# Decoding two weight tiles of an MLP during the attention that stands before it

## The chip, the cores and the metric

The kernel runs on one core of one Trainium2 chip, in one launch. The metric is the device time of one execution in microseconds; lower is better. Three executions of the kernel before took 1065.11, 1061.65 and 1064.87 us, the median is 1064.87 us.

The engines are called by their names in the profile: PE is TensorE (matrix products), DVE is VectorE, ACT is ScalarE, POOL is GpSimd, and SP is the queue that issues all DMA transfers here.

## The reference

Attention with a feature map of exponentials, then two mixer blocks, each of which mixes tokens and then channels. Cut to what is computed:

```python
def phi(x):                      # 64 -> 256 features
    proj = einsum('bhsd,df->bhsf', x, w_phi)
    proj = proj - max(abs(proj), axis=-1)
    return concatenate([exp(proj), exp(-proj)], axis=-1)
num = phi(q) @ (phi(k).T @ v)    # 4 batches, 8 heads, 576 tokens, 64 wide
den = phi(q) @ sum(phi(k)) + 1e-6
x = heads_side_by_side(num / den)            # 4 x 576 x 512
u  = x + (x.T @ U @ V).T                     # token mix, rank 32
x  = u + relu(u @ w_ch1) @ w_ch2             # first channel MLP, 512 -> 2048 -> 512
u2 = x + (relu(x.T @ w_tok1) @ w_tok2).T     # token mix, 576 -> 256 -> 576
out = u2 + relu(u2 @ w2_ch1) @ w2_ch2        # second channel MLP, 512 -> 1536 -> 512
```

## The kernel before, in words

**Numbers.** Every product is made with operands that are split into a high and a low part, and is the sum of three: high by high, high by low, low by high. All weights of the MLPs and mixes reach the chip as 64-bit words. `load64` brings one half tile (128 x 512 words, 512 KB) by DMA into a buffer `raw` (L148) and makes single precision of it: two ACT instructions write `w` and `r` (L153, L154), two DVE instructions join them (L156, L159). `load_half` then calls `split`: ACT casts the high part (`wh`, L99), POOL or DVE subtracts for the low part (`wl`, L104). One weight tile of a hidden slice is two such halves, one for the up and one for the down product, each with a high and a low part.

**Stages.** Stage A works on 16 pairs of heads (4 batches of 4 pairs), one pair in five rounds. A table of rounds (`at(r, fn)`) holds the calls in program order: projections, `k1` to `k3` for the keys, `q1` and `q2` for the queries, `x0`, `xr` and `x1` for the division (the denominators go through DRAM, `rD` and `rec`, L405 to L418), then per batch the rank-32 token mix (`tm0`, `tm1`, `tm2`) and the first 5 of the 16 hidden slices of the first channel MLP (`ma_u`, `ma_h`, `ma_y`), whose weights `a0` to `a4` stand in the pool `wring`. Results go to DRAM as `uD` and `sD`. The last batch's mix and MLP part run after the last heads. `uha`, `ula` and `hp_a` belong to that part, `uhb`, `ulb`, `hp_b` and `yb` to stage B.

Stage B takes the other 11 slices (`b0` to `b10`) for eight half batches of 288 tokens (`channel`), and after each second half `tokmix2`, the second block's token mix; names there are `gp`, `gh`, `gl`, `m2p`, and `x2` is the sum, which goes to DRAM as `u2D`. The first tiles have a pool of their own each (`wrB0` ...), the last ones reuse `wring`. Stage B's decoding of the first READY=8 tiles is issued behind the last `rec` transfer (`tc.issue_after(recl[0])`).

Stage C is the second channel MLP in five chunks of 256 and four times 512 tokens (`channelC`). Its weights are made by `pair_weights` for six pairs of slices, `sh`, `sl` (up) and `vh`, `vl` (down) for each, in pools `wc0` to `wc5` that lie where stage B's pools on the right-hand side lay, so each waits for the last reader of what it lies over. The first chunk, with `u0c`, `u1c`, `hpc`, `hhc`, `hlc`, `yc`, takes the pairs in order as they are decoded; the later ones use combinations of quarters (`t0c` to `t6c`, `u2c`, `xc`).

**Order.** Nothing runs in the order in which the calls stand: a scheduler in the build lays out each engine's instructions by its own simulated times, with the calls' order as priority. `issue_after` holds a call back behind a named instruction. Each engine then works its list strictly in order.

Of the kernel before, what the change touches and what calls it, by code (L numbers as in the profile page):

```python
# [30 lines left out]
NF1 = 16  # L31
NF2 = 12
NA = 5
NR = NF2 - NA
EPS = 1e-06
CHUNKS = (256, 512, 512, 512, 512)
HM = 256
EARLY = 2
READY = 8


NF32 = 4
# [50 lines left out]
def body(ctx, tc, kq, vd, w_phi, U, V, wm1, wt1, wt2, wm2, out):  # L93
# [12 lines left out]
    def split(src, hi, lo, eh, el):  # L106
        cp(eh, hi, src)
        sub(el, lo, src, f32(hi))
# [24 lines left out]
    AB = ExitStack()  # L133
    stage = AB.enter_context(tc.tile_pool(name="stage", bufs=RAWB))
    mlp = AB.enter_context(tc.tile_pool(name="mlp", bufs=2))
    wring = AB.enter_context(tc.tile_pool(name="wring", bufs=NA))

    halves, extra = [], []

# [24 lines left out]
    def load_half(src, i, name, k, hi, lo):  # L164
        sl = slice(k * C, (k + 1) * C)
        w = load64(src[i][:, sl], P, C, f"{name}_{k}")
        split(w, hi[:, sl], lo[:, sl], WHI[name[0]][k], WLO[name[0]][k])

    def w_tiles(pool, name, slot=""):
        return [pool.tile([P, 2 * C], F32R, tag=f"{t}{slot}", name=f"{t}_{name}") for t in ("wh", "wl")]  # L170

    def load_w(pool, src, i, name, slot=""):
        hi, lo = w_tiles(pool, name, slot)
        for k in range(2):
            load_half(src, i, name, k, hi, lo)
        return hi, lo
# [69 lines left out]
    def at(r, fn, *args):  # L246
        rounds.setdefault(r, []).append((fn, args))
# [153 lines left out]
    recs, pks, subs, exps = {}, {}, [], []  # L401
# [75 lines left out]
    def load_wa(f, k):  # L477
        if k == 0:
            wA.append(w_tiles(wring, f"a{f}"))
        with tc.issue_after(subs[-1]), tc.issue_after(exps[-1]):  # L480
            load_half(wm1, f, f"a{f}", k, *wA[f])

    uhl, hss, ys = {}, {}, {}

    def ma_u(b, ch):
# [45 lines left out]
    at(O_MIX, mix_consts)  # L531
    for h in range(2 * NA):
        at(O_WA + (h * D_WA) // 2, load_wa, h // 2, h % 2)
    span = 5 * NPAIR
    for b in range(B):
        r = span * b + 5 * (NPAIR - 1) + O_TM
# [17 lines left out]
    with tc.using_default_side("right"):  # L554
        wrB = [BX.enter_context(tc.tile_pool(name=f"wrB{f}", bufs=1, reuse_waits="tile")) for f in range(NR)]
        extra.append(BX.enter_context(tc.tile_pool(name="rawx", bufs=RAWX, reuse_waits="tile")))
# [6 lines left out]

    nB = NF1 - NA
    def load_b(f):
        if f < NR:
            return load_w(wrB[f], wm1, NA + f, f"b{f}", f)
        return load_w(wring, wm1, NA + f, f"b{f}")

    with tc.issue_after(recl[0]):  # L570
        wB = [load_b(f) for f in range(READY)]

# [59 lines left out]
    def load_u(src, nm, *where):  # L632
        u = mlp.tile(list(src.shape), F32, tag="xT", name=f"u{nm}")
        nc.sync.dma_start(u, src)
        uh, ul = split_u(u, nm, *where)
        return u, uh, ul
# [3 lines left out]
    def mix2_consts():  # L640
        T1H = bc.tile([P, NT, 256], F32R, name="T1H")
        T1L = bc.tile([P, NT, 256], F32R, name="T1L")
        for t in range(NT):
            w = load64(wt1[:, t], P, 256, f"t1_{t}")
            split(w, T1H[:, t], T1L[:, t], "v", "v")
        T2H = bc.tile([P, 2, S], F32R, tag="T2H", name="T2H")
        T2L = bc.tile([P, 2, S], F32R, tag="T2L", name="T2L")
        for j in range(2):
            for k in range(2):
                sl = slice(k * N, (k + 1) * N)  # L650
                w = load64(wt2[:, j, sl], P, N, f"t2_{j}_{k}")
                split(w, T2H[:, j, sl], T2L[:, j, sl], "v", "v")
        return T1H, T1L, T2H, T2L

    for b in range(B):
        x2 = b2.tile([P, NC, S], F32, tag="x2", name=f"x2_{b}", bufs=1)
        for ch in range(2):
            nm = f"b{b}_{ch}"
            i = 2 * b + ch
            u, uh, ul = load_u(uD[i], nm) if i else u0  # L660
            xc = x2[:, :, ch * N : (ch + 1) * N]
            nc.sync.dma_start(xc, sD[i])
            nc.vector.tensor_add(xc, xc, u)
            channel(wB, uh, ul, xc, xc, nm)
            if i == 0:
                T1H, T1L, T2H, T2L = mix2_consts()
        tokmix2(b, x2, T1H, T1L, T2H, T2L)

# [277 lines left out]
```

## Time and profile before

| | us |
|---|---|
| median of three executions | 1064.87 |
| lowest, highest | 1061.65, 1065.11 |
| the profiled execution | 1064.01 |
| its span, from first to last instruction | 1062.2 |
| busy PE, DVE, ACT, POOL | 1015.5, 631.5, 448.5, 240.2 |
| mean granted clock of PE | 0.988 |

The profiled execution spends 1.81 us outside its span. Stage A's heads end near 356 us, the last batch's mix follows until about 385, stage B ends near 770, and stage C fills the rest. A row of a timeline names the start, the length, the engine, the line, the operands (output before the arrow) and in brackets how long the engine was idle before and what ended that. Instructions of one engine overlap a little, so the distance of two starts can be shorter than a length.

### The profile page before, as it was taken

What the parts mean: (1) busy time and instruction counts of PE and PEld (TensorE: products, weight loads), DVE (VectorE), ACT (ScalarE), POOL (GpSimd) and SP (SyncE); (2) the same over time, 40 slices, a digit from 0 to 9 for tenths busy, and PEclk for the clock granted to TensorE, in tenths of its full rate; (3) what the DMA queues carried; (4) which work ended last, traced back from release to release, by engine and by line L of the source; (5) the groups of instructions that cost most, each with busy time, mean ns of one, the idle gap of its engine ahead of it and who ended that gap; (6) DMA issues with size and microseconds to landing.
All of it is one profiled execution on the core that took longest, in us unless ns stands there. A gap on an engine that the chain in (4) does not pass through costs nothing.

```text
span 1062.2 us, 17389 instructions
## 1 busy us (share of the span) xinstructions
PE 1015.5 (96%) x6828; PEld 948.6 (89%) x6828; DVE 631.5 (59%) x1117; ACT 448.5 (42%) x1039; POOL 240.2 (23%) x186
## 2 busy tenths in 40 slices
PE   8988999899989799999999999999899999999998
PEld 6767899799989689999999999998898898988897
DVE  6778867786686596834223323327888763644633
ACT  6766665655655567522112012115673321312211
POOL 3217655555555134100000000003260000000000
PEclk9999999999999899999999999999899999999999
DMA  7532331232231587410300300202753030020201
GB/s 217 159 101 64 106 89 55 81 90 81 73 100 57 169 270 240 125 60 11 102 23 1 112 23 2 89 1 86 249 157 109 2 102 18 19 102 1 80 1 40
DMA packets 59266, 92.15 MB, mean 87 GB/s; under 512 B 14512, under 2 KB 38832, under 8 KB 59184
## 3 DMA queue, kind: packets, MB, share of 16 engines
q1 hardware_dynamic: 59184, 91.03, 27.3%
q8 instruction: 54, 0.88, 0.4%
q14 instruction: 28, 0.23, 0.1%
HBM read 71.99 MB, written 18.95 MB: 86 GB/s over the span
## 4 chain that ended last, share of the span: by engine, by line
PE 75%; DVE 9%; ACT 6%; DMA 4%; issue 3%; POOL 2%; SPq 1%; ACTq 0%; DVEq 0%; POOLq 0%
PE yc L111 14%; PE yb L111 11%; PE hp_b L111 11%; PE pp L111 5%; PE hp_a L111 4%; PE yp L111 4%; PE nm L111 4%; PE kvp L111 3%; PE vc L111 3%; PE zc L111 3%; PE xc L111 3%; PE m2p L111 2%; DMA raw_a<-in_wm_dram 2%; PE gp L111 2%; DVE w_b L159 1%
## 5 line engine op out<-in xcount | busy, mean ns | idle before, releaser
L194 ACT ACTIVATE hhb<-hp_b 128x288 fp32r<-128x288 f32 x88 | 35.9, 408 | 198.2 <-PE hp_b L111 195.5
L195 DVE SCALAR_TENSOR_TENSOR hlb<-hp_b,hhb 128x288 fp32r<-128x288 f32 x88 | 40.0, 455 | 129.1 <-ACT hhb L194 129.1
L111 PE MATMUL hp_b<-ulb,wh_b 128*128 128x288 f32 x352 | 104.0, 296 | 0.0
L111 PE MATMUL hp_b<-uhb,wl_b 128*128 128x288 f32 x352 | 104.0, 296 | 0.0
L111 PE MATMUL hp_b<-uhb,wh_b 128*128 128x288 f32 x352 | 103.4, 295 | 0.0
L111 PE MATMUL yb<-hlb,wh_b 128*128 128x288 f32 x352 | 97.9, 298 | 2.9 <-DVE hlb L195 2.7
L104 POOL TENSOR_TENSOR sl<-w_c,sh 128x256 fp32r<-128x256 f32 (+1 forms) x18 | 23.5, 1326 | 326.3 <-ACT sh L99 326.3
L111 PE MATMUL yb<-hhb,wl_b 128*128 128x288 f32 x352 | 97.1, 295 | 0.0
L111 PE MATMUL yc<-hlc,vh 128*128 128x512 f32 (+1 forms) x240 | 88.6, 373 | 0.0
L111 PE MATMUL yc<-hhc,vl 128*128 128x512 f32 (+1 forms) x240 | 88.3, 373 | 0.0
L111 PE MATMUL pp<-KW,kq 128*128 128x256 f32 x320 | 82.5, 384 | 2.2 <-issue 1.3
L111 PE MATMUL yc<-hhc,vh 128*128 128x512 f32 (+1 forms) x240 | 81.0, 373 | 0.0
L104 POOL TENSOR_TENSOR qel<-qe,qeh 128x640 fp32r<-128x640 f32 (+1 forms) x48 | 70.1, 1468 | 35.7 <-DVE qeh L101 25.1
L286 DVE TENSOR_REDUCE km<-pp 128x4 f32<-128x512 f32 x80 | 54.9, 686 | 28.1 <-PE pp L111 27.7
L111 PEld LDWEIGHTS yb<-hlb,wh_b 128*128 128x128 f32 x352 | 66.1, 188 | 4.8 <-DVE hlb L195 4.7
L111 PE MATMUL yb<-hhb,wh_b 128*128 128x288 f32 x352 | 67.5, 296 | 0.1
L111 PEld LDWEIGHTS hp_b<-ulb,wh_b 128*128 128x128 f32 x352 | 66.2, 188 | 0.3
L111 PEld LDWEIGHTS hp_b<-uhb,wh_b 128*128 128x128 f32 x352 | 66.1, 188 | 0.2
L111 PEld LDWEIGHTS yb<-hhb,wl_b 128*128 128x128 f32 x352 | 66.3, 188 | 0.0
L111 PEld LDWEIGHTS pp<-KW,kq 128*128 128x128 f32 x320 | 57.7, 192 | 9.6 <-issue 1.7
L111 PEld LDWEIGHTS hp_b<-uhb,wl_b 128*128 128x128 f32 x352 | 66.1, 188 | 0.0
L104 POOL TENSOR_TENSOR kel<-ke,keh 128x512 fp32r<-128x512 f32 x36 | 51.4, 1438 | 46.4 <-ACT keh L99 41.1
(242 smaller groups left out, 2892.9 us busy)
## 6 DMA issues: line engine op xcount, KB each, us to landing
raw_c<-in_wm_dram SPq DMA_DIRECT2D x24, 512.0 KB, 4.5
raw_b<-in_wm_dram SPq DMA_DIRECT2D x22, 512.0 KB, 5.3
kq<-in_kq_dram SPq DMA_DIRECT2D x80, 128.0 KB, 2.2
raw_a<-in_wm_dram SPq DMA_DIRECT2D x10, 512.0 KB, 4.3
rec<-rD SPq DMA_DIRECT2D x32, 144.0 KB, 3.1
uD<-xT SPq DMA_DIRECT2D x8, 576.0 KB, 4.2
sD<-ys SPq DMA_DIRECT2D x8, 576.0 KB, 3.9
ub<-uD SPq DMA_DIRECT2D x8, 576.0 KB, 3.7
```

Source lines behind the costliest of these rows:

```text
L104: return ENG[e].tensor_tensor(out=o, in0=a, in1=b, op=ALU.subtract)
L111: return nc.tensor.matmul(o, l, r, start=start, stop=stop, skip_group_check=True)
L159: nc.vector.scalar_tensor_tensor(out=wi, in0=top, scalar=-(2**31), in1=wi, op0=ALU.bitwise_and, op1=ALU.bitwise_or)
L194: a = nc.scalar.activation(hh, hp, AF.Relu)
L195: v = nc.vector.scalar_tensor_tensor(out=hl, in0=hp, scalar=0.0, in1=f32(hh), op0=ALU.max, op1=ALU.subtract)
L286: nc.vector.tensor_reduce(out=m, in_=pv, op=ALU.max, axis=AX.X, apply_absolute_value=True)
```

## The change

The pool `wring` grows from 5 to 7 tiles, and the pools `wrB` shrink from 7 to 5. The main tiles b0 and b1 are loaded and decoded by `load_we` in four halves, which stand in the table at rounds 74, 78, 82 and 86, that is during the last two pairs of heads and the mix behind them. Stage B's own loading begins at b2. After the first half batch the list of weights is turned, so that later half batches take b2 to b10 first and b0 and b1 last. The count of decode instructions stays the same.

```diff
--- before.py
+++ after.py
@@ -31,12 +31,15 @@
 NF1 = 16
 NF2 = 12
 NA = 5
-NR = NF2 - NA
+NE = 2
+NR = NF2 - NA - NE
 EPS = 1e-06
 CHUNKS = (256, 512, 512, 512, 512)
 HM = 256
 EARLY = 2
 READY = 8
+O_WB = 74
+D_WB = 4
 
 
 NF32 = 4
@@ -133,7 +136,7 @@
     AB = ExitStack()
     stage = AB.enter_context(tc.tile_pool(name="stage", bufs=RAWB))
     mlp = AB.enter_context(tc.tile_pool(name="mlp", bufs=2))
-    wring = AB.enter_context(tc.tile_pool(name="wring", bufs=NA))
+    wring = AB.enter_context(tc.tile_pool(name="wring", bufs=NA + NE))
 
     halves, extra = [], []
 
@@ -480,6 +483,14 @@
         with tc.issue_after(subs[-1]), tc.issue_after(exps[-1]):
             load_half(wm1, f, f"a{f}", k, *wA[f])
 
+    wE = []
+
+    def load_we(f, k):
+        if k == 0:
+            wE.append(w_tiles(wring, f"b{f}"))
+        with tc.issue_after(subs[-1]), tc.issue_after(exps[-1]):
+            load_half(wm1, NA + f, f"b{f}", k, *wE[f])
+
     uhl, hss, ys = {}, {}, {}
 
     def ma_u(b, ch):
@@ -531,6 +542,8 @@
     at(O_MIX, mix_consts)
     for h in range(2 * NA):
         at(O_WA + (h * D_WA) // 2, load_wa, h // 2, h % 2)
+    for h in range(2 * NE):
+        at(O_WB + h * D_WB, load_we, h // 2, h % 2)
     span = 5 * NPAIR
     for b in range(B):
         r = span * b + 5 * (NPAIR - 1) + O_TM
@@ -563,8 +576,10 @@
 
     nB = NF1 - NA
     def load_b(f):
-        if f < NR:
-            return load_w(wrB[f], wm1, NA + f, f"b{f}", f)
+        if f < NE:
+            return wE[f]
+        if f < NE + NR:
+            return load_w(wrB[f - NE], wm1, NA + f, f"b{f}", f - NE)
         return load_w(wring, wm1, NA + f, f"b{f}")
 
     with tc.issue_after(recl[0]):
@@ -663,6 +678,7 @@
             nc.vector.tensor_add(xc, xc, u)
             channel(wB, uh, ul, xc, xc, nm)
             if i == 0:
+                wB[:] = wB[NE:] + wB[:NE]
                 T1H, T1L, T2H, T2L = mix2_consts()
         tokmix2(b, x2, T1H, T1L, T2H, T2L)
```

What the scheduler makes of it is shown at three places. Buffer numbers stand behind the names, line numbers of the kernel after are larger by 3 and more.

The first is POOL at the last pair of heads (pair 15). `keh`, `qel` are its key and query features, `wl_b` low parts of weights. Before:

```order
L104 TENSOR_TENSOR keh15_4_4241<-ke15_4_4238,keh15_4_4241 64x512
L104 TENSOR_TENSOR qel15_0_0_4264<-qe15_0_0_4260,qeh15_0_0_4263 128x640
L104 TENSOR_TENSOR qel15_1_0_4275<-qe15_1_0_4271,qeh15_1_0_4274 128x640
L104 TENSOR_TENSOR qel15_0_1_4324<-qe15_0_1_4320,qeh15_0_1_4323 128x2x256
L104 TENSOR_TENSOR qel15_1_1_4334<-qe15_1_1_4330,qeh15_1_1_4333 128x2x256
L104 TENSOR_TENSOR wl_b0_5089<-w_b0_0_5092,wh_b0_5088 128x512
L104 TENSOR_TENSOR wl_b0_5089<-w_b0_1_5102,wh_b0_5088 128x512
```

After:

```order
L107 TENSOR_TENSOR keh15_4_4263<-ke15_4_4260,keh15_4_4263 64x512
L107 TENSOR_TENSOR wl_b0_4005<-w_b0_1_4225,wh_b0_4004 128x512
L107 TENSOR_TENSOR qel15_0_0_4286<-qe15_0_0_4282,qeh15_0_0_4285 128x640
L107 TENSOR_TENSOR qel15_1_0_4297<-qe15_1_0_4293,qeh15_1_0_4296 128x640
L107 TENSOR_TENSOR wl_b1_4413<-w_b1_0_4416,wh_b1_4412 128x512
L107 TENSOR_TENSOR qel15_0_1_4346<-qe15_0_1_4342,qeh15_0_1_4345 128x2x256
L107 TENSOR_TENSOR qel15_1_1_4356<-qe15_1_1_4352,qeh15_1_1_4355 128x2x256
L107 TENSOR_TENSOR wl_b1_4413<-w_b1_1_4506,wh_b1_4412 128x512
```

Two weight subtractions now stand among the features of the last pair, one ahead of its first query feature and one ahead of its third.

The second is ACT behind the heads, where `xh3` are the last batch's transposed tokens and `rh3` the cast that the rank-32 mix waits for. Before:

```order
L358 CAST xh3_3_4532<-xp3_3_4527 128x512
L355 CAST xh3_4_4560<-xp3_4_4555 64x512
L154 ACTIVATE r_b2_0_5137<-raw_b2_0_5134 128x512
L153 ACTIVATE w_b1_1_5124<-raw_b1_1_5122 128x512
L99 CAST wh_b1_5110<-w_b1_0_5114 128x512
L154 ACTIVATE r_b2_1_5147<-raw_b2_1_5144 128x512
L99 CAST rh3_4581<-rp3_4476 128x512
```

After:

```order
L361 CAST xh3_3_4576<-xp3_3_4571 128x512
L358 CAST xh3_4_4604<-xp3_4_4599 64x512
L157 ACTIVATE r_b4_0_5175<-raw_b4_0_5172 128x512
L156 ACTIVATE w_b3_1_5162<-raw_b3_1_5160 128x512
L102 CAST wh_b3_5148<-w_b3_0_5152 128x512
L102 CAST rh3_4625<-rp3_4520 128x512
```

The cast `rh3` no longer stands behind an `r_b` that waits for an older decode; three weight instructions instead of four stand between the tokens and it.

The third is the start of stage C, on ACT, with `w_c`, `r_c`, `sh2`, `vh2` of the weights, `u0c0` the first chunk's input, `gh3` the last token mix. Before:

```order
L355 CAST xh23_4_8613<-x2p3_4_8608 64x512
L99 CAST sh2_8848<-w_c4_0_8854 128x512
L154 ACTIVATE r_c4_1_8877<-raw_c4_1_8874 128x512
L99 CAST u0c0_9034<-uc0_9032 128x1024
L99 CAST sh2_8848<-w_c5_0_8864 128x256 x2
L194 ACTIVATE gh3_8620<-gp3_0_8546 128x512
L153 ACTIVATE w_c5_1_8886<-raw_c5_1_8884 128x512
L194 ACTIVATE gh3_8620<-gp3_1_8547 128x512
L154 ACTIVATE r_c5_1_8887<-raw_c5_1_8884 128x512
L99 CAST vh2_8850<-w_c4_1_8876 128x512
L153 ACTIVATE w_c6_0_8900<-raw_c6_0_8898 128x512
L194 ACTIVATE hhc0_0_0_9059<-hpc0_0_0_9046 128x256
```

After:

```order
L358 CAST xh23_4_8607<-x2p3_4_8602 64x512
L157 ACTIVATE r_c4_1_8869<-raw_c4_1_8866 128x512
L102 CAST u0c0_9026<-uc0_9024 128x1024
L197 ACTIVATE gh3_8614<-gp3_0_8540 128x512
L197 ACTIVATE gh3_8614<-gp3_1_8541 128x512
L157 ACTIVATE r_c5_1_8879<-raw_c5_1_8876 128x512
L197 ACTIVATE hhc0_0_0_9051<-hpc0_0_0_9038 128x256
L197 ACTIVATE hhc0_0_1_9068<-hpc0_0_1_9055 128x256
L197 ACTIVATE hhc0_1_0_9092<-hpc0_1_0_9079 128x256
L102 CAST sh2_8840<-w_c4_0_8846 128x512
L102 CAST sh2_8840<-w_c5_0_8856 128x256 x2
L102 CAST vh2_8842<-w_c4_1_8868 128x512
```

The casts `sh2` and `vh2` moved from ahead of and among `u0c0` and `gh3` to behind three `hhc0`; `wc2` now lies over buffers that the last token mix reads. DVE at the same place, before:

```order
L104 TENSOR_TENSOR u1c0_9035<-uc0_9032,u0c0_9034 128x1024
L195 SCALAR_TENSOR_TENSOR gl3_8621<-gp3_0_8546,gh3_8620 128x512
L195 SCALAR_TENSOR_TENSOR gl3_8621<-gp3_1_8547,gh3_8620 128x512
L156 SCALAR_TENSOR_TENSOR w_c5_1_8886<-w_c5_1_8886,r_c5_1_8887 128x512
L159 SCALAR_TENSOR_TENSOR w_c5_1_8886<-raw_c5_1_8884,w_c5_1_8886 128x512
L195 SCALAR_TENSOR_TENSOR hlc0_0_0_9060<-hpc0_0_0_9046,hhc0_0_0_9059 128x256
L156 SCALAR_TENSOR_TENSOR w_c6_0_8900<-w_c6_0_8900,r_c6_0_8901 128x512
L159 SCALAR_TENSOR_TENSOR w_c6_0_8900<-raw_c6_0_8898,w_c6_0_8900 128x512
L629 TENSOR_TENSOR x2_3_7875<-m2p3_0_0_8626,x2_3_7875 128x288
L629 TENSOR_TENSOR x2_3_7875<-m2p3_0_1_8634,x2_3_7875 128x288
L104 TENSOR_TENSOR vl2_8851<-w_c5_1_8886,vh2_8850 128x512
L629 TENSOR_TENSOR x2_3_7875<-m2p3_0_2_8642,x2_3_7875 128x288
```

After:

```order
L198 SCALAR_TENSOR_TENSOR hlc0_0_1_9069<-hpc0_0_1_9055,hhc0_0_1_9068 128x256
L644 TENSOR_TENSOR x2_3_7869<-m2p3_0_0_8620,x2_3_7869 128x288
L644 TENSOR_TENSOR x2_3_7869<-m2p3_0_1_8628,x2_3_7869 128x288
L644 TENSOR_TENSOR x2_3_7869<-m2p3_0_2_8636,x2_3_7869 128x288
L644 TENSOR_TENSOR x2_3_7869<-m2p3_0_3_8644,x2_3_7869 128x288
L198 SCALAR_TENSOR_TENSOR hlc0_1_0_9093<-hpc0_1_0_9079,hhc0_1_0_9092 128x256
L644 TENSOR_TENSOR x2_3_7869<-m2p3_1_0_8653,x2_3_7869 128x288
L644 TENSOR_TENSOR x2_3_7869<-m2p3_1_1_8661,x2_3_7869 128x288
L644 TENSOR_TENSOR x2_3_7869<-m2p3_1_2_8669,x2_3_7869 128x288
L644 TENSOR_TENSOR x2_3_7869<-m2p3_1_3_8677,x2_3_7869 128x288
L159 SCALAR_TENSOR_TENSOR w_c5_1_8878<-w_c5_1_8878,r_c5_1_8879 128x512
L162 SCALAR_TENSOR_TENSOR w_c5_1_8878<-raw_c5_1_8876,w_c5_1_8878 128x512
```

The decoding of c5_1, c6_0 and c7_0 now stands behind the last of the eight `x2_3` sums.

## Rows read from the trace of the kernel before

**Rows 1.** The page's first part: busy us and share of each engine, instructions.
```profile
PE 1015.5 (96%) x6828; PEld 948.6 (89%) x6828; DVE 631.5 (59%) x1117; ACT 448.5 (42%) x1039; POOL 240.2 (23%) x186
```

**Rows 2.** The page's fourth part: the chain that ended last, shares by engine.
```profile
PE 75%; DVE 9%; ACT 6%; DMA 4%; issue 3%; POOL 2%; SPq 1%; ACTq 0%; DVEq 0%; POOLq 0%
```

**Rows 3.** Windows: stretch, length, then busy us (instructions) per engine, granted clock, DMA share, GB/s.
```profile
310.00:356.00 46.00, 46.00 (x342) 45.28 (x341) 27.75 (x47) 23.85 (x62) 20.52 (x15) 1.00 0.20 64
355.00:385.00 30.00, 20.32 (x106) 16.50 (x105) 25.61 (x33) 20.35 (x36) 8.09 (x6) 0.83 0.76 244
757.00:758.00 1.00, 0.00 (x0) 0.00 (x0) 1.00 (x1) 1.00 (x3) 0.32 (x2) 0.72 0.34 98
758.00:764.00 6.00, 5.79 (x26) 5.80 (x27) 4.54 (x8) 2.88 (x6) 1.28 (x1) 0.50 0.78 223
785.00:810.00 25.00, 22.22 (x179) 21.19 (x179) 22.74 (x44) 13.41 (x30) 7.91 (x5) 1.00 0.22 66
```

**Rows 4.** Timeline, VectorE, end of an early weight decode: start, length, line, operands.
```profile
69.58 0.69 DVE L159 SCALAR_TENSOR_TENSOR w_a<-raw_a,w_a 128x512 int32<-128x512 int32 x1
```

**Rows 5.** Timeline, SP queue, the same place.
```profile
70.30 0.46 SPq L417 DMA_DIRECT2D rec<-rD  x1
```

**Rows 6.** Timeline, GpSimd, the first main weight's subtraction.
```profile
362.01 1.29 POOL L104 TENSOR_TENSOR wl_b<-w_b,wh_b 128x512 fp32r<-128x512 f32 x1 [15.41 <-ACT wh_b L99]
```

**Rows 7.** Waits of TensorE from 355 to 385: what for, total us, times, longest.
```profile
PE rp L111 <- ACT xh L358: 3.4, 1, 3.4
PE mp L111 <- ACT rh L99: 2.3, 1, 2.3
```

**Rows 8.** Timeline, ScalarE, after the heads.
```profile
358.30 0.66 ACT L153 ACTIVATE w_b<-raw_b 128x512 f32<-128x512 f32 x1 [3.08 <-DMA raw_b<-in_wm_dram]
...
370.24 0.67 ACT L154 ACTIVATE r_b<-raw_b 128x512 int32<-128x512 uint32 x1 [1.92 <-DVE w_b L156]
370.94 0.58 ACT L99 CAST rh<-rp 128x512 fp32r<-128x512 f32 x1
```

**Rows 9.** Timeline, VectorE, the same stretch.
```profile
354.97 1.54 DVE L428 TENSOR_TENSOR xT<-nd,rec 64x576 f32<-64x576 f32 x2 [3.27 <-DMA rec<-rD]
```

**Rows 10.** Waits of TensorE from 700 to 812.
```profile
PE xc L111 <- DVE u2c L838: 1.6, 1, 1.6
PE hpc L111 <- DVE u1c L104: 1.3, 1, 1.3
...
PE m2p L111 <- ACT gh L194: 0.7, 1, 0.7
```

**Rows 11.** Timeline, TensorE, the last token-mix products.
```profile
764.69 0.29 PE L111 MATMUL m2p<-T2H,gh 128*128 128x288 f32 x1
764.82 0.29 PE L111 MATMUL m2p<-T2L,gh 128*128 128x288 f32 x1
```

**Rows 12.** Timeline, ScalarE, start of the second channel MLP.
```profile
770.40 1.23 ACT L99 CAST sh<-w_c 128x512 fp32r<-128x512 f32 x3 [2.12 <-PE m2p L111]
```

**Rows 13.** VectorE groups from 771 to 803: count, busy us, mean ns, idle before.
```profile
L159 DVE SCALAR_TENSOR_TENSOR w_c<-raw_c,w_c 128x512 int32<-128x512 int32 x10 | 9.8, 979 | 0.1
L156 DVE SCALAR_TENSOR_TENSOR w_c<-w_c,r_c 128x512 int32<-128x512 int32 x9 | 8.2, 908 | 1.9 <-ACT w_c L153 1.9
L195 DVE SCALAR_TENSOR_TENSOR hlc<-hpc,hhc 128x256 fp32r<-128x256 f32 x9 | 3.7, 414 | 0.5 <-ACT hhc L194 0.5
...
L725 DVE TENSOR_TENSOR s<-sh,sl 128x256 f32<-128x256 f32 x4 | 1.7, 419 | 0.4 <-POOL sl L104 0.4
```

**Rows 14.** GpSimd groups, the same stretch.
```profile
L104 POOL TENSOR_TENSOR sl<-w_c,sh 128x256 fp32r<-128x256 f32 (+1 forms) x9 | 13.0, 1473 | 20.4 <-ACT sh L99 20.4
L104 POOL TENSOR_TENSOR vl<-w_c,vh 128x512 fp32r<-128x512 f32 x3 | 4.9, 1647 | 1.9 <-ACT vh L99 1.8
```

**Rows 15.** Timeline, VectorE, two undisturbed decode operations.
```profile
787.34 0.68 DVE L159 SCALAR_TENSOR_TENSOR w_c<-raw_c,w_c 128x512 int32<-128x512 int32 x1
787.95 0.68 DVE L156 SCALAR_TENSOR_TENSOR w_c<-w_c,r_c 128x512 int32<-128x512 int32 x1
```

## The prediction

> **What bounds the kernel now.** I read the page's busy times first: TensorE works in 96% of the span, VectorE in 59%, the rest less [rows 1]. The chain of waits comes next: 75% of it is TensorE, then 9% VectorE, 6% ScalarE, 4% DMA [rows 2]. So other engines cost time only where TensorE waits, and the windows say where that is. From 310 to 356 us, the last pairs of heads, TensorE is busy in 46.00 of 46 us while VectorE works 27.75, ScalarE 23.85 and GpSimd 20.52. From 355 to 385, behind the heads, it stands idle for 30 − 20.32 = 9.68 us. At 757 to 758 it does nothing and its granted clock falls to 0.72, and from 758 to 764 it is busy for 5.79 us at 0.50, the lower of its two levels. From 785 to 810 it is idle for 25 − 22.22 = 2.78 us with VectorE busy 22.74 of 25 [rows 3]. These are the stretches that a move of weight decoding can touch. The heads are a stretch without idle time, where work on the other engines can be had free but where a delay shows only once it exceeds their slack.
>
> **The change part by part.** The count of decode instructions is the same; everything is a matter of place. Sums are made against the profiled execution, 1064.01 us, which is its span of 1062.2 and 1.81 outside.
>
> *Early transfers.* The two raw halves of b0 now stand in SP's queue among the early pairs, one ahead of a denominator's store and one ahead of its `rec`. Each waits for a raw buffer, the second for the one whose decode ends at 69.58 + 0.69 = 70.27; the `rec` behind it was issued at 70.30 anyway [rows 4, 5]. What is left is one issue in front of it. I take +0.5; the bounds are −0.5 and +2, should the wait for the buffer push the division back.
>
> *Decoding among the last heads.* Of each half, GpSimd does a subtraction of 1.29 us [rows 6], where it is not VectorE that does it, VectorE two operations and ScalarE three, of about 0.6 each [rows 8, 15]. Four halves lie in a stretch where TensorE hides them. Two things are not hidden. One `wl_b1` stands ahead of the third query feature of the last pair, so 1.3 us are added to GpSimd's chain, and in TensorE's list the last product of that pair (`nm`) now stands behind twelve further matrix products of 0.13 us, 1.6 us [rows 11]. The last pair's division feeds `xT`, which VectorE reached after 3.27 us of waiting for `rec` [rows 9], so the end of the heads is a chain of latencies, and what delays the last `nm` delays the transition. I take +1.8, a little over the larger of the two, since both lie partly beside one another; the bounds are −0.5, if the slack of the heads swallows both, and +3, if they add.
>
> *Behind the heads.* TensorE's two largest waits here are 3.4 us for `xh` and 2.3 us for `rh` [rows 7]. `xh` stands behind the first main weight's `w_b`, which waited 3.08 us for its DMA. The list of after still has a `w_b2`, `r_b2` ahead of it, so this wait stays, for the same transfer issued at the same place. `rh` waited because the `r_b` ahead of it stood idle for 1.92 us for a VectorE operation [rows 8]. In the new list that `r_b` stands behind `rh`, and one decode operation fewer stands between the tokens and it: −1.6 of the 1.92 and −0.6, so −2.2. The bounds are 0, if an older decode holds ScalarE up anyway, and −4, if half of the wait for `xh` goes too.
>
> *Start of stage C.* The narrower `wrB` pools shift what lies above them, and `wc2` now lies over `gh`, `gl` and the mix's matrices. Its casts move behind three `hhc`. Ahead of the last mix the way is then clear: the waits for `gh` (0.7) and `u1c` (1.3) go [rows 10], −2.0. If TensorE is not stopped at 757, the clock does not fall, and 5.79 us of work at half the clock become 2.9 [rows 3], with the tail after 764 −3.0. Eight more `hpc` stand ahead of the mix's end, 8 × 0.13 = +1.0 by the spacing of the next larger product [rows 11]. The mix ends 4.0 earlier.
>
> In exchange VectorE's decoding of c5_1, c6_0, c7_0 and the first operation of c6_1 now stands behind the last sum of `x2`: 7 operations that start 0.61 apart [rows 15] are 4.3, one low part 0.6. They meet GpSimd's subtractions. In the stretch from 771 to 803 the two decode groups take 979 and 908 ns where 680 are undisturbed: 10 × 0.30 + 9 × 0.23 = 5.0 us, against twelve GpSimd operations, 0.42 for each [rows 13 to 15]. Four more such operations move in, +1.7. Against 4.3 + 0.6 + 1.7 = 6.6 stand VectorE's idle times there, 1.9 + 0.5 + 0.4 = 2.8 [rows 13], so +3.8, on the engine that TensorE follows from 785 to 810. `sh` of the fourth pair waited 2.12 us for the last mix product [rows 12]; `wc2` takes that role now, and the third pair comes at the time of the fourth. Last, `u2c`, for which TensorE waited 1.6 [rows 10], stands earlier in VectorE's list by five rows; I take −1.0. Stage C is then −4.0 + 3.8 − 1.0 = −1.2. The bounds are −5.0, if the deferred decoding is hidden, and +5.6, if the clock falls anyway and all of it is paid: −2.0 + 1.0 + 6.6 and no gain at `u2c`.
>
> The Trainium skill, page "SBUF — State Buffer", section "SBUF: two separate sides", has VectorE operations with two inputs in SBUF and GpSimd share a pair of ports as an exclusive lock, where the later one is blocked for the whole instruction of the other. By it the four collisions could cost the full 1.29 each, 5.1 in place of 1.7, and the sum would be 3.4 higher, still nearly the time before. The trace agrees in kind, a decode of 0.68 becomes up to 0.98 on average, but not in size: 0.42 for each GpSimd operation, since not every one finds a decode.
>
> *Sum.* 0.5 + 1.8 − 2.2 − 1.2 = −1.1. From the profiled execution that gives 1062.9, from the median of 1064.87 it gives 1063.8. I forecast 1063.3.
>
> **The rivals.** *Faster, weights no bound in stage C.* VectorE's deferred decoding is hidden, because TensorE has first-chunk products to do between pairs and the clock is full: 0.5 + 1.8 − 2.2 − 5.0 = −4.9, 1059.1. For it speaks that TensorE loses only 2.78 us from 785 to 810 [rows 3]; against it, that VectorE is busy in 22.74 of these 25 us and has nowhere to put 6.6 more.
>
> *Slower, the third pair's weights come too late.* `sl2` and `vh2` wait for the last product of the mix, GpSimd and VectorE begin there with all that was done beside the mix before, and TensorE runs dry in the first chunk. TensorE then also stops long enough for its clock to fall once more, so that the gain at 758 to 764 is lost: 0.5 + 1.8 − 2.2 + 5.6 = +5.7, 1069.7. It decides where the deferred work exceeds the gain of 4.0 and the idle 2.8 together, 6.8, against 6.6 as estimated: a narrow margin. For it speaks that 1.00 us without a product came right before six at 0.50 [rows 3]; against it, that VectorE had 1.9 us of waiting in the group to be filled [rows 13].
>
> The Trainium skill, page "TensorE: Matmul & The Clock Gate", section "HAM oscillation — how this bites in real kernels", says that waits for data between stretches of matrix products make the next stretch begin at the low clock. It is this rival's rule: by it the slowdown at 758 comes back wherever the weights run late. The trace shows it once, 757 to 764.
>
> *The heads pay.* The transition gains nothing because the last pair ends 3 us later and `rh` waits on another weight instruction: 0.5 + 3 − 0 − 1.2 = +2.3, 1066.3. This stays in the measurement's noise.
>
> **How the numbers follow.** A measurement of this kernel can tell about 0.3% from no change, 3.2 us, so 1061.7 to 1068.1. The forecast's own case (0.40) and the paying heads (0.10) lie within. The faster rival has 0.30, the slower one 0.20. The forecast's terms add some spread to either side: faster 0.33, the same 0.45, slower 0.22. The range reaches from 1058.5, just under the faster rival, to 1069.0, over most of the way to the slower one, and leaves out the worst of it.
>
> **What would show it.** In the profile after: from 310 to 356 TensorE busy throughout, the last `nd` copy later by 1 to 2 us; from 355 to 385 no wait for `rh` above 0.7, and the one for `xh` as before; the granted clock at 1.00 from 757 to 764 with the last `m2p` some 4 us earlier relative to stage B's end; a wait of ScalarE's `sh` or GpSimd's `sl` of the third pair for `m2p`; and TensorE idle for longer than 2.8 us in the first chunk of stage C. The forecast is wrong if the clock still falls there, if TensorE waits over 5 us for `hlc` or `sl` in stage C, or if idle time shows up inside the heads.

## The result and the profile after

The changed kernel takes 1077.28 us (median of six executions, 1075.42 to 1081.52) against 1062.03 (six, 1059.40 to 1065.11): a ratio of 1.0137, interval 1.0119 to 1.0155. Forecast were 1063.3 and a range up to 1069.0. The change makes the kernel about 15 us slower.

The profiled execution is the slowest of the six, 1081.52 us, with a span of 1079.7. Its busy times, and its chain by engine and line, answer to [rows 1, 2]:

```profile
PE 1023.6 (95%) x6828; PEld 954.4 (88%) x6828; DVE 632.3 (59%) x1117; ACT 449.9 (42%) x1039; POOL 236.8 (22%) x186
...
PE 73%; DVE 12%; DMA 7%; ACT 4%; issue 3%; POOL 1%; SPq 0%; DVEq 0%; POOLq 0%; ACTq 0%
PE yc L114 14%; PE hp_b L114 10%; PE yb L114 10%; PE yp L114 5%; PE pp L114 5%; PE hp_a L114 4%; PE nm L114 4%; PE kvp L114 3%; PE vc L114 3%; PE zc L114 3%; PE xc L114 3%; PE m2p L114 2%; PE gp L114 2%; DMA x<-sD 2%; DVE w_c L159 1%
```

The work is the same, but VectorE's share of the chain rises from 9 to 12%, and `w_c`, a weight decode of stage C, now stands by name among the chain's lines.

To see where the time went I took, from the timelines of ScalarE, the starts of instructions that both kernels have: the 17th and the 89th of the 96 `qe` exponentials, the last `nd` copy (the end of the heads), the 6th and the last of the 88 `hhb` (stage B), the third and the last of the 84 `hhc` (stage C). In before they start at 126.6, 337.4, 347.9, 431.7, 741.9, 767.3 and 1051.0 us. The table gives how much longer each stretch takes than there, for all kernels of this study (each from its one profiled execution):

| kernel | to 17th `qe` | to 89th | to last `nd` | to 6th `hhb` | to last `hhb` | to 3rd `hhc` | to last `hhc` | sum |
|---|---|---|---|---|---|---|---|---|
| after | +6.6 | +0.1 | +7.5 | −0.1 | +0.1 | −5.4 | +8.6 | +17.5 |
| e1_layout_only | +0.8 | 0.0 | 0.0 | +2.2 | −0.2 | −5.4 | +8.6 | +6.1 |
| e3_gate_raw | −1.5 | −1.1 | +2.1 | −0.1 | −0.4 | −5.4 | +8.6 | +2.3 |
| e4_relayout | +1.4 | +0.1 | +7.7 | −5.3 | +0.1 | −4.8 | +9.7 | +8.8 |
| e5_gate_relayout | +4.3 | −1.1 | +2.2 | −0.9 | −0.3 | −4.9 | +8.5 | +7.9 |
| f_pad | +9.1 | −1.1 | +7.7 | −5.2 | −0.1 | −4.8 | +0.2 | +5.8 |
| g_pad_gate | −0.7 | +0.1 | +2.1 | −0.1 | −0.7 | −4.8 | +0.2 | −3.8 |
| l_ownraw | +4.1 | +1.2 | +7.7 | −0.7 | −0.3 | −5.4 | +8.6 | +15.2 |
| h_before_pad | +2.1 | −1.1 | 0.0 | −0.6 | +0.2 | −2.7 | +0.2 | −1.9 |
| m_early_b0 | +3.6 | −1.1 | +2.2 | −0.3 | −0.5 | −4.9 | +0.2 | −0.7 |
| p_spread | +0.8 | +2.9 | 0.0 | −2.2 | −0.3 | −4.9 | +0.3 | −3.3 |
| q_64 | +6.1 | −0.4 | +0.5 | −0.2 | −0.6 | −4.8 | +0.2 | +0.7 |
| s_xh_first | −0.2 | +0.5 | +0.5 | −2.4 | −0.1 | −4.8 | +0.5 | −5.9 |

The stretches from the 89th `qe` on repeat to a few tenths wherever the schedule is the same; the one before it varies by about 1.2. The first does not repeat at all: g_pad_gate and q_64 have the same schedule there and show −0.7 and +6.1, and most kernels' executions lie 4 to 10 us apart. So a single profile says nothing about the first stretch, and the medians are needed. Of the changed kernel's 17.5, the table puts 7.5 on the end of the heads and 8.6 − 5.4 = 3.2 on stage C. The rest is the first stretch.

**The heads.** Windows of after around the last pair, with the columns of [rows 3], and its longest waits from 345 to 400, with those of [rows 7]:

```profile
320.00:349.00 29.00, 28.98 (x213) 28.23 (x211) 22.63 (x34) 20.95 (x52) 19.33 (x14) 1.00 0.23 70
350.00:354.00 4.00, 0.25 (x2) 0.00 (x0) 3.49 (x3) 1.46 (x4) 2.80 (x3) 0.94 0.37 152
354.00:357.00 3.00, 2.88 (x12) 2.88 (x13) 2.81 (x6) 0.00 (x0) 0.41 (x1) 0.51 0.02 5
```

```profile
PE rp L114 <- ACT xh L361: 4.2, 2, 3.3
PE hp_a L114 <- DVE hla L198: 3.9, 1, 3.9
PE xp L442 <- DVE xT L431: 1.6, 1, 1.6
...
PE mp L114 <- DVE rl L107: 0.8, 1, 0.8
PE mp L114 <- ACT rh L102: 0.7, 1, 0.7
```

TensorE stands still for almost 4 us and then works at the lower clock, 0.51, for three more. In before this stretch had no idle time [rows 3]. It waits for `hla`, so the next view is VectorE's timeline there:

```profile
342.80 0.68 DVE L162 SCALAR_TENSOR_TENSOR w_b<-raw_b,w_b 128x512 int32<-128x512 int32 x1
...
344.00 0.16 DVE L415 TENSOR_SCALAR pk<-pk 128x9 f32<-128x9 f32 x1
344.07 0.68 DVE L159 SCALAR_TENSOR_TENSOR w_b<-w_b,r_b 128x512 int32<-128x512 int32 x1
...
344.80 1.66 DVE L162 SCALAR_TENSOR_TENSOR w_b<-raw_b,w_b 128x512 int32<-128x512 int32 x1
...
350.51 1.52 DVE L431 TENSOR_TENSOR xT<-nd,rec 64x576 f32<-64x576 f32 x1 [3.25 <-DMA rec<-rD]
351.96 1.74 DVE L159 SCALAR_TENSOR_TENSOR w_b<-w_b,r_b 128x512 int32<-128x512 int32 x1
353.62 0.44 DVE L198 SCALAR_TENSOR_TENSOR hla<-hp_a,hha 128x288 fp32r<-128x288 f32 x1
```

and GpSimd's beside it:

```profile
344.27 1.63 POOL L107 TENSOR_TENSOR wl_b<-w_b,wh_b 128x512 fp32r<-128x512 f32 x1 [2.54 <-ACT wh_b L102]
...
351.77 1.38 POOL L107 TENSOR_TENSOR qel<-qe,qeh 128x512 fp32r<-128x512 f32 x1 [0.35 <-ACT qeh L102]
```

`pk` of the last but one pair (344.00) stands behind a decode. Behind it come two decode operations, then `xT`, which waits 3.25 us for `rec`, and a decode operation of 1.74 us. Only then, at 353.62, comes the `hla` that TensorE needs. Two decode operations here take 1.66 and 1.74 us in place of 0.68 [rows 15], beside GpSimd's subtractions of 1.63 and 1.38. The Trainium skill, page "SBUF — State Buffer", section "SBUF: two separate sides", has the one of the two that comes later blocked for the other's whole instruction. These rows agree: each of the two began while a subtraction was running (344.80 behind 344.27, 351.96 behind 351.77), and it is 1.0 us longer each time, most of the subtraction. The mean of 0.42 that I took for stage C is the wrong price for an operation on a path, and for the heads I had taken none.

**Stage C.** GpSimd and ScalarE in after, then windows of after, then the waits of TensorE from 755 to 830 (those of before: [rows 10]):

```profile
780.45 2.69 POOL L107 TENSOR_TENSOR sl<-w_c,sh 128x512 fp32r<-128x512 f32 x3 [27.62 <-PE m2p L114]
...
781.77 0.67 ACT L156 ACTIVATE w_c<-raw_c 128x512 f32<-128x512 f32 x1 [0.80 <-POOL sl L107]
```

```profile
758.00:770.00 12.00, 11.40 (x67) 9.37 (x66) 9.51 (x16) 8.94 (x15) 0.00 (x0) 1.00 0.76 259
770.00:780.00 10.00, 10.00 (x82) 10.00 (x81) 5.67 (x13) 2.27 (x6) 0.00 (x0) 1.00 0.72 245
...
800.00:815.00 15.00, 11.53 (x65) 10.55 (x64) 14.90 (x19) 10.71 (x21) 8.26 (x7) 0.77 0.31 93
```

```profile
PE yc L114 <- ACT vh L102: 2.1, 1, 2.1
PE yc L114 <- ACT hhc L197: 1.4, 1, 1.4
PE yc L114 <- DVE hlc L198: 1.1, 1, 1.1
```

The mix does end earlier: its clock stays at 1.00 and the waits for `u1c` and `gh` are gone. The last `m2p` of before, then of after, to be read against the last `hhb` at 741.93 and 756.14:

```profile
770.20 0.29 PE L111 MATMUL m2p<-T2H,gl 128*128 128x288 f32 x1
...
780.02 0.29 PE L114 MATMUL m2p<-T2H,gl 128*128 128x288 f32 x1
```

It starts 28.3 us behind `hhb` in before and 23.9 in after, 4.4 sooner; from it to the last `hhc` after takes 7.7 us longer. (The table's −5.4 and +8.6 divide the same 3.2 at the third `hhc`.) GpSimd is idle for 27.62 us, until the last `m2p`, before the third pair's `sl`, and ScalarE's next decode, `w_c` at 781.77, waits for that `sl` to set a buffer free. VectorE has 5.67 us of work in the ten before 780, and is then busy in 14.90 of 15 from 800, where TensorE has 11.53 and the clock falls to 0.77.

### The profile page after: what moved, and what is told of

Its sections match the earlier page's. It is cut to its first block, busy times and chain, and to the rows that moved or that the text cites. A ratio compares the mean times of both kernels' runs of the same rounds, so it can differ in the third digit from the quotient of the medians.

```text
span 1079.7 us, 17376 instructions
## 1 busy us (share of the span) xinstructions
PE 1023.6 (95%) x6828; PEld 954.4 (88%) x6828; DVE 632.3 (59%) x1117; ACT 449.9 (42%) x1039; POOL 236.8 (22%) x186
## 4 chain that ended last, share of the span: by engine, by line
PE 73%; DVE 12%; DMA 7%; ACT 4%; issue 3%; POOL 1%; SPq 0%; DVEq 0%; POOLq 0%; ACTq 0%
PE yc L114 14%; PE hp_b L114 10%; PE yb L114 10%; PE yp L114 5%; PE pp L114 5%; PE hp_a L114 4%; PE nm L114 4%; PE kvp L114 3%; PE vc L114 3%; PE zc L114 3%; PE xc L114 3%; PE m2p L114 2%; PE gp L114 2%; DMA x<-sD 2%; DVE w_c L159 1%
## 5 line engine op out<-in xcount | busy, mean ns | idle before, releaser
L107 POOL TENSOR_TENSOR sl<-w_c,sh 128x256 fp32r<-128x256 f32 (+1 forms) x18 | 20.8, 1178 | 333.2 <-ACT sh L102 305.6
```

The costliest lines, as they stand in the source:

```text
L107: return ENG[e].tensor_tensor(out=o, in0=a, in1=b, op=ALU.subtract)
```

## The experiments

Three theories stood against each other: three separate losses (early pairs, last heads, stage C); all of it from the layout of stage C; all of it from decoding among the heads. A ratio is to before, with its interval.

**e1_layout_only**: the pools and the turned list, without the early decoding.

```diff
-    for h in range(2 * NE):
-        at(O_WB + h * D_WB, load_we, h // 2, h % 2)
...
-            return wE[f]
+            return load_w(wring, wm1, NA + f, f"b{f}")
```

> The pools and the turned list of weights as in the changed kernel, but b0 and b1 decoded at the start of stage B as before. Theory of three parts (a transfer and decodes among the early pairs, a late division in the last pairs, deferred decoding in stage C): only the third part is left, so about +3 us against before, with the last m2p some 4 us earlier after stage B than before and TensorE idle longer in the first chunk of stage C; heads and transition as before. Rival, all of the loss comes from where stage C's weights lie: +12 to +15 us. Rival, the layout is harmless: within 1.5 us of before.

Measured 1069.90 us against 1063.35, ratio 1.0059 (1.0038 to 1.0081). The layout with the turned list costs +6: the +3.2 of stage C, exactly as in the changed kernel, and +2.2 in the transition, which none of the theories had. Neither "harmless" nor "all of it".

**e3_gate_raw**: the early transfers held behind the last `rec`.

```diff
-        with tc.issue_after(subs[-1]), tc.issue_after(exps[-1]):
+        with tc.issue_after(subs[-1]), tc.issue_after(exps[-1]), tc.issue_after(recl[0]):
             load_half(wm1, NA + f, f"b{f}", k, *wE[f])
```

> The changed kernel, but each of the four early raw transfers is held behind the last rec transfer issued so far, so none stands among the early pairs and none right ahead of a denominator's store. Theory of three parts: the first two go, so +2 to +5 us against before, no stop of TensorE for hla near 350 us. Rival, the decoding work itself does not fit among the last heads, wherever its transfers stand: +9 to +12 us, with TensorE idle in the last pair again. Rival, all in stage C: +12 to +15.

Measured 1069.77, ratio 1.0064 (1.0042 to 1.0085), about the same as e1: above the theory's +2 to +5 and below both rivals. The stop for `hla` is gone, as the theory had it, and the heads lose 2.1 instead of 7.5. The hold moved the transfers, and with them the decodes of b1, which now stand behind `hla` in VectorE's list, so it does not yet tell the two apart. Windows from the 89th `qe` to the last `nd`, of before, after and this kernel:

```profile
337.40:347.89 10.49, 10.49 (x83) 10.40 (x82) 5.57 (x9) 6.51 (x19) 6.24 (x4) 1.00 0.23 86
...
344.04:362.06 18.02, 13.73 (x95) 13.24 (x94) 10.03 (x17) 9.30 (x25) 10.06 (x7) 0.91 0.23 80
...
334.80:347.12 12.32, 12.32 (x98) 12.32 (x97) 7.23 (x14) 8.13 (x21) 7.62 (x5) 1.00 0.43 116
```

Here TensorE is busy throughout, at the full clock. It does 98 products between the two marks in place of 83, so what the heads still lose is products that now stand ahead of the last `nm`, and no wait.

**l_ownraw**: the second half of b1 has a raw buffer of its own and loads near the start; the decodes keep their places.

```diff
+    early = AB.enter_context(tc.tile_pool(name="early", bufs=1))
...
-            load_half(wm1, NA + f, f"b{f}", k, *wE[f])
+            load_half(wm1, NA + f, f"b{f}", k, *wE[f], rawin="e" if (f, k) == (1, 1) else None)
```

> The changed kernel, but the raw half that stood right ahead of the last but one pair's denominator (second half of b1) has a raw buffer of its own and is loaded near the start; the decodes keep their places on VectorE and ScalarE. Theory, that transfer of 512 KB made rec late, and with it hla, for which TensorE stopped for 3.87 us: the heads end 4 us or more earlier against the changed kernel, +8 to +11 us against before. Rival, the decodes ahead of the denominator and of hla on VectorE are what made it late: the wait for hla near 350 us stays above 2 us, +13 to +16.

Measured 1078.35, ratio 1.0138 (1.0124 to 1.0152): the same as the changed kernel. The heads lose 7.7 again. The theory of the late transfer falls. Its wait and VectorE's timeline ahead of it:

```profile
PE hp_a L114 <- DVE hla L201: 2.8, 1, 2.8
```

```profile
342.62 0.16 DVE L418 TENSOR_SCALAR pk<-pk 128x9 f32<-128x9 f32 x1
...
343.41 1.66 DVE L165 SCALAR_TENSOR_TENSOR w_b<-raw_b,w_b 128x512 int32<-128x512 int32 x1
...
345.80 2.05 DVE L162 SCALAR_TENSOR_TENSOR w_b<-w_b,r_b 128x512 int32<-128x512 int32 x1
347.80 2.08 DVE L434 TENSOR_TENSOR xT<-nd,rec 64x576 f32<-64x576 f32 x1
349.80 1.75 DVE L165 SCALAR_TENSOR_TENSOR w_b<-raw_b,w_b 128x512 int32<-128x512 int32 x1
351.48 0.44 DVE L201 SCALAR_TENSOR_TENSOR hla<-hp_a,hha 128x288 fp32r<-128x288 f32 x1
```

No 512 KB stand ahead of the store any more, and `xT` comes 1.3 us sooner behind `pk` (5.2 us against 6.5 in after) and no longer waits for `rec`, but the decode operations, 1.66, 2.05 and 1.75 us long, hold `hla` until 351.48. What costs is the decodes' place in VectorE's list.

**e4_relayout** and **e5_gate_relayout**: the right-hand pools in another order, without and with the hold of e3.

```diff
+        bx = BX.enter_context(tc.tile_pool(name="bx", bufs=2, reuse_waits="tile"))
+        bt = BX.enter_context(tc.tile_pool(name="bt", bufs=1, reuse_waits="tile"))
         bc = BX.enter_context(tc.tile_pool(name="bc", bufs=1, reuse_waits="tile"))
...
-            xh, xl = split_tokens(xp, b2, f"2{b}_{t}", t)
+            xh, xl = split_tokens(xp, bx, f"2{b}_{t}", t)
...
-        T1H = bc.tile([P, NT, 256], F32R, name="T1H")
+        T1H = bt.tile([P, NT, 256], F32R, name="T1H")
```

> The changed kernel with the right-hand pools in another order: the token tiles xh, xl and the matrix T1 lie between the raw buffers and the rest, so the third pair's weights no longer lie over what the last token mix reads. Theory of three parts: stage C no longer loses and keeps the earlier end of the mix, 3 to 7 us less than the changed kernel, so +8 to +12 us against before. Rival, stage C's order is not what costs: as the changed kernel, +14 to +16.

> Both at once: transfers held behind rec, and the other order of the right-hand pools. Theory of three parts: all three losses go and the shorter transition and the earlier end of the mix remain, -6 to 0 us against before. Rival, decoding among the last heads costs by itself: +4 to +8.

Measured 1072.55, ratio 1.0085 (1.0068 to 1.0102), and 1069.38, 1.0056 (1.0037 to 1.0075). The third pair comes in time, but stage C still loses 4.9 and 3.6. That e4's total lies inside the theory's +8 to +12 is luck: what it gains is 5.3 in the transition, not in stage C. e5 fell outside what the theory gave and into its rival's range, but by stage C and not by the heads (+2.2). ScalarE of e4 says why:

```profile
777.75 1.23 ACT L102 CAST sh<-w_c 128x512 fp32r<-128x512 f32 x3 [3.03 <-DMA u2D<-x]
```

The fourth pair's `sh` now waits for a transfer, the store of `x2`: in this order its pool lies over `x2`. The wait had moved one pair on. This left open whether the layout was the cause in stage C at all.

**f_pad** and **g_pad_gate**: 8 KB of unused room and the token tiles moved beside it, so that the mix's buffers begin where they began in before; again without and with the hold.

```diff
+        pad = BX.enter_context(tc.tile_pool(name="pad", bufs=1, reuse_waits="tile"))
+        pad.tile([P, 8 * 256], F32, tag="pad", name="pad")
+        bx = BX.enter_context(tc.tile_pool(name="bx", bufs=2, reuse_waits="tile"))
         bc = BX.enter_context(tc.tile_pool(name="bc", bufs=1, reuse_waits="tile"))
...
-            xh, xl = split_tokens(xp, b2, f"2{b}_{t}", t)
+            xh, xl = split_tokens(xp, bx, f"2{b}_{t}", t)
```

> The changed kernel with 8 KB of unused room and the token tiles xh, xl between the raw buffers and the last token mix's buffers, so that these begin at the same distance as before and the third pair's weights lie over nothing that the mix's last products read. Theory, stage C loses because the third pair's weights wait for the last m2p and VectorE stands idle meanwhile: from the last hhb to the last hhc the changed kernel loses 3.3 us against before; here it should gain 1 to 4, so +7 to +10 us against before in all. Rival, the order of the first chunk with its earlier mix is what costs: stage C loses 3 to 5 again, +12 to +15 in all.

> The same room, and the early raw transfers held behind rec. Theory: nothing of the loss is left, -4 to +2 us against before, stage C 1 to 4 shorter than before, heads and transition together within 2 us of before. Rival, decoding in the last heads costs by itself: +4 to +7.

Measured 1065.69, ratio 1.0019 (1.0005 to 1.0033), and 1061.06, 0.9981 (0.9969 to 0.9992). The room and the moved token tiles take 12 us from the changed kernel. Stage C is 4.6 shorter than before, not 3.2 longer; this is what the edit was made for. The transition is 5.2 shorter, which no expectation had, and by this the total fell below the theory's +7 to +10. There the scheduler laid out another order: ScalarE in after, then in f_pad, and f_pad's wait from 355 to 405:

```profile
372.85 0.66 ACT L156 ACTIVATE w_b<-raw_b 128x512 f32<-128x512 f32 x1 [3.06 <-DMA raw_b<-in_wm_dram]
...
373.96 0.58 ACT L361 CAST xh<-xp 128x512 fp32r<-128x512 f32 x1
...
372.75 0.59 ACT L361 CAST xh<-xp 128x512 fp32r<-128x512 f32 x1 [1.43 <-PE xp L442]
374.29 0.68 ACT L156 ACTIVATE w_b<-raw_b 128x512 f32<-128x512 f32 x1 [0.95 <-DMA raw_b<-in_wm_dram]
```

```profile
PE rp L114 <- ACT xh L361: 1.0, 3, 0.7
```

The first `xh` stands ahead of the `w_b` that waits for its transfer, and TensorE waits 1.0 us for `xh` in place of 4.2. With the hold that order, and the gain, are gone again (−0.1). GpSimd and the windows of f_pad for stage C, to be read beside those of after; f_pad's last `hhb` is 3.9 us earlier, and so are its windows:

```profile
765.88 3.03 POOL L107 TENSOR_TENSOR sl<-w_c,sh 128x512 fp32r<-128x512 f32 x3 [16.91 <-ACT sh L102]
...
777.52 3.15 POOL L107 TENSOR_TENSOR sl<-w_c,sh 128x512 fp32r<-128x512 f32 x3 [6.91 <-ACT sh L102]
```

```profile
766.10:776.10 10.00, 10.00 (x83) 10.00 (x82) 9.38 (x18) 7.25 (x15) 4.51 (x4) 1.00 0.79 274
...
796.10:811.10 15.00, 12.40 (x100) 11.79 (x100) 14.97 (x24) 7.59 (x17) 4.51 (x4) 1.00 0.13 36
```

The third pair's `sl` starts at 765.88, released by `sh` and no longer by the last `m2p`. VectorE works 9.38 us in the ten where it had 5.67, and later the clock stays at 1.00 where it fell to 0.77. With the hold, the kernel is 0.2% faster than before.

**h_before_pad**: the same in before, with 11 KB of room.

> The kernel before, with 11 KB of unused room and the token tiles xh, xl between the raw buffers and the last token mix's buffers, so that the fourth pair's weights need not wait for the last m2p. Theory, VectorE's decoding is what the first chunk of stage C runs after: 1 to 3 us faster than before, without the 2.12 us wait of sh for m2p. Rival, TensorE is the bound there and decoding was early enough: within 1 us.

Measured 1062.11, ratio 0.9989 (0.9977 to 1.0000). The edit did not do what it was made for: the fourth pair's `sh` still waits for the last `m2p`.

```profile
768.42 1.24 ACT L99 CAST sh<-w_c 128x512 fp32r<-128x512 f32 x3 [2.25 <-PE m2p L111]
```

Stage C is 2.5 shorter in the profile all the same, for another reason. Windows of before, then of this kernel, each from 11 to 16 and from 16 to 22 us behind the last `hhb`:

```profile
752.93:757.93 5.00, 3.01 (x14) 2.06 (x14) 4.95 (x4) 4.97 (x10) 4.29 (x4) 0.95 0.60 192
757.93:763.93 6.00, 5.72 (x26) 5.73 (x27) 4.61 (x8) 2.95 (x6) 1.35 (x1) 0.50 0.77 222
...
753.53:758.53 5.00, 3.02 (x14) 2.06 (x14) 4.93 (x5) 4.98 (x10) 4.25 (x4) 1.00 0.60 202
758.53:764.53 6.00, 5.72 (x46) 5.72 (x47) 5.90 (x12) 3.49 (x8) 1.38 (x1) 1.00 0.76 238
```

TensorE does the same 14 products and then stands idle as long, but here its clock stays at 1.00 afterwards, where it fell to 0.50 in before. So neither the theory nor the rival is tested, and the gain in the medians is not clear of nothing. No other profile of this study has the fall at this place, and each kernel has one profile: whether other executions of before have it, no run shows. So some 2.7 of every −5.4 to −4.8 in the table may belong to before's one execution.

**m_early_b0**: g_pad_gate, with only b1's transfers held.

```diff
+        with ExitStack() as held:
+            for ins in [subs[-1], exps[-1]] + [recl[0]] * (f > 0):
+                held.enter_context(tc.issue_after(ins))
```

> As the kernel with room and held transfers (0.998 of before), but the two raw halves of b0 are no longer held: they stand among the early pairs again, as in the changed kernel, and the schedule differs from that kernel only between the third and the sixth pair. Theory, these two transfers and what they displace cost in the early pairs: 2 to 5 us slower than that kernel, so +0 to +3 against before, all of it there by 130 us. Rival, the early differences between the profiles are chance from execution to execution: within 1 us of that kernel, -3 to -1 against before.

Measured 1063.39, ratio 1.0000 (0.9984 to 1.0017), 1.9 per mille above g_pad_gate, about 2 us, at the lower end of the theory. The intervals of the two overlap slightly, so the loss in the early pairs is likely and not shown.

**p_spread** and **q_64**: g_pad_gate with other rounds.

```diff
-O_WB = 74
-D_WB = 4
+O_WB = 42     # q_64: 64
+D_WB = 8      # q_64: 3
```

> As the kernel with room and held transfers, but the four halves stand at rounds 42, 50, 58 and 66, away from the last pairs. Theory, decoding is free where the engines beside TensorE have slack and no latency chain ends: the 2.2 us that the last heads still lost go, so -5 to -2 us against before. Rival, a decode costs wherever it lies in the heads, since VectorE is busy for 74 of 100 us there: -1 to +2.

> The same with rounds 64, 67, 70 and 73, just ahead of the last pair. Theory: as the spread one, -5 to -2 us against before, if what counts is only to be done before the last pair's division. Rival, close together they hold up the pairs before: -1 to +2.

Measured 1061.48, ratio 0.9987 (0.9969 to 1.0005), and 1059.69, 0.9977 (0.9959 to 0.9994). In both the end of the heads loses at most 0.5 instead of 2.1. In p_spread's profile the decodes cost 2.9 in the pairs where they now lie; in q_64's, just ahead of the last pair, they do not. q_64 lies where its theory had it. p_spread, −1.4, lies between its theory and its rival, and the intervals of the two kernels overlap, so the medians do not tell the two places apart.

**s_xh_first**: q_64, with stage B's loading also held behind the last batch's first token cast (`xhl` is a list of these casts).

```diff
-    with tc.issue_after(recl[0]):
+    with tc.issue_after(recl[0]), tc.issue_after(xhl[4 * (B - 1)]):
```

> As the kernel with rounds 64 to 73 (0.998 of before), but stage B's loading is also held behind the first token cast xh of the last batch, so this cast no longer stands behind a weight's w_b2 on ScalarE. Theory, TensorE's wait of 3.4 us for xh in the transition is the wait for that weight's transfer: the wait falls under 1 us and the kernel is 2 to 4 us faster than the one with rounds 64 to 73, -6 to -4 against before. Rival, the cast only moves the wait to rh or to the first weights of stage B: within 1 us of it, -3 to -1.5.

Measured 1058.79 against 1061.90, ratio 0.9969 (0.9957 to 0.9982), about 3 us faster than before and so faster than both kernels. Its waits in the transition, beside [rows 7]:

```profile
PE rp L114 <- ACT xh L363: 2.7, 3, 1.2
...
PE mp L114 <- ACT rh L102: 0.7, 1, 0.7
```

The longest wait for `xh` falls from 3.3 in q_64 to 1.2, but there are three now, and the transition gains 2.2 against q_64 in the table. By the medians the kernel is 0.9 faster than q_64, as the rival had it, and against before it lies just past the rival's −3. Part of the wait moved on.

## Why the prediction was wrong

The forecast was −1.1 us, as 0.5 − 2.2 + 1.8 − 1.2. By its steps:

- *Early transfers*, +0.5 forecast: likely +2 (m_early_b0 against g_pad_gate), at the upper bound given.
- *Decoding among the last heads*, +1.8 forecast with a bound of +3: +7.5 measured. This is the step that failed most. I priced GpSimd's subtraction and twelve products of TensorE, and counted VectorE's decode operations as hidden because VectorE had 27.75 us of work in 46. The twelve products were right: TensorE does 95 instead of 83 between the marks, 1.6 us at 0.13 each. At nothing I had put the rest. TensorE is idle for 18.02 − 13.73 = 4.3 of the 18.02 us, and of its 13.73 busy us, 3.2 more than in before, about 1.7 are neither the old products nor the twelve: an estimate of what the clock cost, which fell to 0.51 behind the stop. The order had decode operations ahead of `pk`, `xT` and `hla`, a chain that has no slack, and those that met GpSimd's subtractions took 1.7 to 2.0 us. l_ownraw shows that it is their place, e3_gate_raw that 5.4 of the 7.5 go when b1's stand behind `hla`.
- *Behind the heads*, −2.2 forecast: −0.1. `rh` did fall from 2.3 to 0.7, as predicted, and `xh` stayed. But new waits came, for `xT` (1.6) and `rl` (0.8), and took it back. That the schedule there was worth 5 us is shown by f_pad and e4_relayout, with the same end of the heads and −5.2 and −5.3; 3.2 of it is the wait for `xh`, which I had forecast to stay, as it does in after.
- *Start of stage C*, −4.0 for the mix: −4.4 at the last `m2p`, right in kind and size. The clock stays up and the waits go, in every kernel with that order. But −3.0 of it was the clock, whose fall I put down to TensorE's stop at 757, and h_before_pad has that stop without the fall. So part of this hit may be luck.
- *Deferred decoding*, +3.8 − 1.0 forecast: +7.7 from the last `m2p` to the last `hhc`. This is the second step that failed. I took VectorE's idle time of 2.8 in the stretch as room. It was not there: VectorE ran 14.90 of 15 us from 800 to 815, and the idle time lay ahead, from 770 to 780, when nothing could be decoded since the buffers hung on the third pair's subtraction. The slower rival had named this place and its cause, with +5.6 for stage C against the 3.2 measured; but it had the clock fall again at the mix, where it stayed up, while it did fall later, to 0.77 from 800 to 815.

So two steps, each about where decode operations stand in VectorE's list, made the sign: 7.5 for 1.8 and 7.7 for 2.8. The faster rival, with −5.0 for stage C, is shown wrong by the +3.2 of after, and f_pad, with −4.6, shows that the place of the buffers is what made the difference. What stays open: what exactly the early pairs cost, and whether before's clock falls at the mix in its other executions. The medians differ by 15.2; 7.5 and 3.2 leave 4.5 of that, of which m_early_b0 makes some 2 likely. If the fall of the clock belongs to before's one profile alone, stage C loses 2.7 more against the median and the sum comes out; this is an estimate that no run shows.

## What to carry to other kernels

An engine's free share in a stretch hides nothing that stands ahead of the instruction on which a chain of latencies hangs: for each added instruction, ask what the next one behind it in the list is needed for, and price it at the length that it is seen to have beside the other engine's instructions, here 1.7 to 2.0 us and not 0.68. When a pool shrinks, what lies above it moves: look up what each later pool lies over afterwards, and whose last read it will wait for. Here 8 KB of unused room, with the token tiles moved beside it, were worth 12 us: some 8 in stage C, as meant, and 5 in the transition, by an order that the scheduler happened to lay out. The early decoding itself brought little even at its best place: 0.9977 for q_64 against 0.9989 for the room in before without it, with intervals that overlap.

## What the runs showed of the hardware

VectorE's decode of 0.68 us took 1.66 to 2.05 us among GpSimd's subtractions in the last pair, and `xT`, which took 0.76 at 354.09 in after, 2.08 in l_ownraw. After the same 14 products and the same idle time, TensorE's granted clock was 0.50 for the next 6 us in before and 1.00 in h_before_pad. Executions of most kernels differ by 4 to 10 us, and in the profiles the difference arises in the first 130 us, while the stretches from there to the end repeat within some tenths.
